# Attention, token mixing and channel mixing on one core: the rows of batch 3 transposed by way of HBM and VectorE instead of TensorE

## The chip, the cores and the metric

The kernel runs on one core of one Trainium2 chip. The metric is the device time of one execution in microseconds (us); the profile's span is some 1.8 us shorter, since it goes from the first to the last instruction. Engines: PE is TensorE (PEld its weight loads), DVE VectorE, ACT ScalarE, POOL GpSimd, SP SyncE, whose queue issues DMAs.

## The reference, cut to what matters

Eight batches, 576 tokens, 8 heads of 64, model width 512. Keys and values are pooled over 8 tokens to 72, attention is computed, and its output x (576 x 512) goes through a token mixing and a channel mixing:

```
xt = x.transpose(0, 2, 1)
h  = np.maximum(xt @ w_tok1, 0.0) @ w_tok2          # mixes tokens
u  = x + h.transpose(0, 2, 1)
h2 = np.maximum(u @ w_ch1, 0.0) @ w_ch2             # mixes channels
return (u + h2).astype(np.float32)
```

The channel mixing contracts over the model width, and the kernel hands u to TensorE with the width on the partitions. The token mixing leaves tokens on the partitions. Each batch's u therefore has to be transposed, 128 x 128 at a time.

## The kernel before

The kernel is written as nine units. Unit n is the channel mixing of batch n: 48 steps, each with two 512-column matmuls, 24 for the first weight (line L512 in the profile of before) and 24 for the second (L534). Unit 8 takes the ninth 64-token piece of every batch, two of which share a tile ("tails"). Into the steps of unit n, a plan weaves the attention of batch n+2 (names with `>`) and the token mixing of batch n+1 (names without). In the timelines each engine's instructions come in the order in which the plan issues them: in run e4 below, VectorE's attention outputs stand behind block transposes that waited 14.2 us.

```
def unit(n, at):
    for i, _ in enumerate(unit_steps(n, ...)):       # two matmuls of the channel mixing, then
        for s in at.get(i, "").split():              # what the plan has at this step
            if s[0] == "l": load(s[1], n + int(s[2])); continue
            ahead = {"<": 0, ">": 2}.get(s[0], 1)
            batches[n + ahead][1][s.lstrip("<>")]()
```

The names that matter: `K V` pool keys and values on GpSimd, `Q0` to `Q3` transpose the queries on VectorE, `kpT` the pooled keys on TensorE, `s0 s1 s2` are score groups, whose exponentials ScalarE takes, `av0` to `av4` the attention outputs (VectorE divides and writes x), `at u` the token mixing, `lq lk lv` load the queries, keys and values of a later batch. There are two ways to transpose u:

```
def uT(c):           # t0..t4: TensorE, then a copy from PSUM
    ps = ps_tr.tile([P, 4, P], BF16, name="pt")                  # this pool has one buffer
    for kk in range(4):
        nc.tensor.transpose(out=ps[:, kk, :], in_=parts(src)[:, kk], identity=ident)
    nc.vector.tensor_copy(out=dst[:, :, o:o + P], in_=ps)

def spill(i):        # M0 M2 M4: u to HBM
    nc.sync.dma_start(out=st["mem"][...], in_=src)
def quads():         # M: back, four DMAs, so that 32x32 blocks lie right
    st["v"] = swap.tile([P, 4 * 5, P], BF16, name="v")           # this pool has one buffer
    for a in range(4):
        nc.sync.dma_start(out=st["v"][32 * a:32 * a + 32, ...],
                          in_=st["mem"][0:n, :, a * P:(a + 1) * P].rearrange("c (i t) f -> t (c i) f", i=4))
def blocks(c):       # T0..T4: VectorE transposes blocks
    nc.vector.transpose(out=dst[...], in_=st["v"][:, 4 * c:4 * c + 4, :]...)
```

Batches 4 to 7 take the second way, batches 1 to 3 the first (batch 0 has one of its own).

The softmax here doesn't subtract the row's maximum and nothing guards it: scores larger than these inputs give would overflow.

Of the kernel before, what the change touches and what calls it, by code (L numbers as in the profile page):

```python
# [20 lines left out]
def kernel(  # L21
# [483 lines left out]
    def unit_steps(n, st):  # L505
# [36 lines left out]
        for a in range(2):  # L542
# [7 lines left out]
            for half in range(2):  # L550
# [9 lines left out]
             11: "lv3", 12: "kpT", 14: "s0", 15: "v1", 19: "s1", 25: "s2", 26: "av0", 27: "av1", 29: "av2",  # L560
             30: ">K1 av4", 31: "av3", 33: "at1", 34: "at0", 35: ">K0", 36: ">V1 u0", 37: "u1", 39: "t0 >V0",
             40: "u2", 41: "t1 u4 u3", 42: "t2", 44: "t3", 46: "t4"}
    SECOND = {0: ">K1 Q0 lq3 kpT Q1 Q2", 1: "lv3", 3: "s0 lk3 >V0", 4: ">K0", 6: "Q3 >V1", 8: "s1", 13: "s2",
              16: "av1 av0", 19: "av2", 20: "av3", 22: "av4", 24: "at1 at0", 26: "u0", 28: ">Q0", 29: "u1", 30: "t0",
              31: "u2", 32: "t1", 33: "u3 t2", 35: "t3", 36: ">Q1", 37: ">kpT", 38: "lq4", 39: ">s0 >Q2",
              40: ">Q3 lv4", 44: ">s1", 45: "lk4"}
    THIRD = {0: ">V0 >K1", 1: "s2", 2: ">K0 >V1", 3: "av0 av1", 6: "av3", 7: "av2", 9: "av4", 10: "at0",
             12: "at1 >Q0", 15: "u0", 16: "u1", 17: "u2 t0", 18: "u4", 19: "t1", 21: "u3", 22: "t2", 24: ">Q1",
             25: "t3", 27: "lq4 >kpT", 28: "lv4", 29: "lk4 >Q3 >s0 >Q2", 32: "t4", 33: ">s1", 38: ">s2", 40: ">av0",
             41: ">av2", 43: ">av1", 45: ">av3", 47: ">av4"}  # L570
    FOURTH = {0: "M4 u4 >K1", 1: "at0 at1 >K0", 3: "u0 >V0", 5: "u1 M0", 6: ">V1", 7: "u2", 8: "u3 M2", 9: "M",
              15: ">kpT >Q1", 17: ">Q0", 22: "lq4", 25: ">Q2", 26: ">s0", 27: "T0", 28: ">Q3 lk4 lv4", 29: "T1",
              32: ">s1 T2", 34: "T3", 37: ">s2", 38: "T4", 39: ">av0", 41: ">av1", 42: ">av2", 45: ">av3", 46: ">av4"}
    LATER = {0: ">K1 at0", 1: "at1", 2: ">V1", 3: "u1 >V0", 5: "u0 u2 u4 >K0", 7: "M0 M4", 9: "u3", 10: "M2", 11: "M",
             14: ">Q0", 17: ">Q1", 20: ">kpT", 22: ">s0", 25: ">Q2", 26: ">Q3", 27: "T0 >s1", 28: "T3", 31: "T2 T1",
             35: ">s2", 37: ">av1 >av0", 38: "T4", 41: ">av2", 45: ">av3", 46: ">av4"}
# [13 lines left out]
    def unit(n, at):  # L590
        if n + 2 < B:
            batches[n + 2][0]()
        for i, _ in enumerate(unit_steps(n, batches[n][2] if n < B else None)):
            for s in at.get(i, "").split():
                if s[0] == "l":
                    load(s[1], n + int(s[2]))
                    continue
                ahead = {"<": 0, ">": 2}.get(s[0], 1)
                s = s.lstrip("<>")
                if n + ahead < B and ((n + ahead) % 2 or s not in ("u4", "t4", "M4", "T4")):  # L600
                    batches[n + ahead][1][s]()

    with tc.manual_schedule(engines={PE, POOLE, DVE, ACT, SYNC}):
# [24 lines left out]
        unit(0, FIRST)  # L628
        unit(1, SECOND)
        unit(2, THIRD)  # L630
        unit(3, FOURTH)
        for n in range(4, B + 1):
# [31 lines left out]
```

## Time and profile before

| | before |
|---|---|
| time, median of 3 first runs | 275.23 us (275.15 to 275.76) |
| span of the profiled run | 273.7 us |
| TensorE busy | 266.1 us, 97% |
| VectorE busy | 52% of the span |
| transposes of u on TensorE (L420) | 56 |
| block transposes on VectorE (L442) | 18 |

The share of busy time does not say what a single instruction costs: matmuls overlap, so 420 of them with a duration of 379 ns each keep TensorE busy for only 101.5 us. The prediction shows the lines of the profile before and reads them.

### The profile page before, as it was taken

How to read it: one execution, taken by the hardware profiler on the slowest of the kernel's cores; microseconds unless marked ns; L12 is line 12 of the kernel's file. 1: busy time of each engine (PE TensorE's matmuls, PEld its weight loads, DVE VectorE, ACT ScalarE, POOL GpSimd, SP SyncE). 2: the span in 40 equal slices, each digit the busy share in tenths (PEclk: the TensorE clock that was granted, in tenths of full speed). 3: DMA queues.
4: the chain of work that ended last, by engine and by line, in shares of the span. 5: the costliest groups of instructions: out<-in, count | busy, mean ns of one | idle time of the engine just before them, and what ended most of it. 6: DMA issues, size and time to landing. Idle time of an engine off the chain costs nothing.

```text
span 273.7 us, 4544 instructions
## 1 busy us (share of the span) xinstructions
PE 266.1 (97%) x1832; PEld 130.4 (48%) x1832; DVE 141.9 (52%) x280; ACT 110.4 (40%) x182; POOL 131.1 (48%) x121
## 2 busy tenths in 40 slices
PE   7799999999999999999999999999999999999994
PEld 3774545544453544454445444544454444444443
DVE  5487677862584666467267627753674062022022
ACT  2443690058306534525641484147413603603600
POOL 8685223999997991899099999300000000000000
PEclk9999999999999999999999999999999999999999
DMA  7999999990976920894399362225223634024024
GB/s 149 195 203 206 205 205 203 227 197 7 175 123 120 220 37 0 140 228 127 77 159 220 94 133 65 61 69 117 52 66 96 125 61 104 0 53 103 2 47 106
DMA packets 36837, 32.68 MB, mean 119 GB/s; under 512 B 14288, under 2 KB 30288, under 8 KB 36816
## 3 DMA queue, kind: packets, MB, share of 16 engines
q0 software_dynamic: 18672, 17.64, 40.7%
q1 hardware_dynamic: 17984, 14.62, 21.1%
q8 instruction: 14, 0.23, 0.3%
q10 hardware_dynamic: 160, 0.13, 0.2%
q14 instruction: 7, 0.06, 0.1%
HBM read 38.21 MB, written 11.80 MB: 183 GB/s over the span
## 4 chain that ended last, share of the span: by engine, by line
PE 89%; DMA 3%; ACT 3%; DVE 2%; POOL 1%; issue 1%; POOLq 0%
PE p L534 33%; PE p L512 32%; PE p L410 6%; PE p L395 6%; PE p L344 3%; PE p L260 3%; DMA vr<-in_v_dram 3%; ACT ex L265 1%; PE pt L420 1%; ACT GT L516 1%; PE p L226 1%; PE p L546 1%; POOL kr L86 1%; PE pt L376 1%; PE p L461 0%
## 5 line engine op out<-in xcount | busy, mean ns | idle before, releaser
L534 PE MATMUL p<-w_ch,GT 128*128 128x512 bf16 x420 | 101.5, 379 | 0.0
L512 PE MATMUL p<-uT,w_ch 128*128 128x512 bf16 x384 | 92.8, 379 | 0.1
L516 ACT ACTIVATE GT<-p 128x512 bf16<-128x512 f32 x108 | 63.8, 598 | 70.4 <-PE p L512 70.0
L512 PEld LDWEIGHTS <-w_ch 128*128 128x128 bf16 x432 | 40.6, 98 | 47.3 <-issue 2.5
L534 PEld LDWEIGHTS <-GT 128*128 128x128 bf16 x420 | 38.0, 98 | 42.0 <-issue 3.3
L520 DVE TENSOR_TENSOR o<-p,u 128x512 f32<-128x512 f32 x32 | 21.9, 685 | 31.6 <-PE p L534 31.2
L265 ACT ACTIVATE ex<-p 72x1024 bf16<-72x1024 f32 (+1 forms) x42 | 31.7, 807 | 13.5 <-PE p L260 13.5
L147 POOL TENSOR_TENSOR t<-t 72x512 f32<-72x512 f32 x24 | 30.4, 1265 | 1.9
L411 DVE TENSOR_TENSOR u<-p,x 128x512 bf16<-128x512 f32 x32 | 21.7, 690 | 14.7 <-PE p L410 14.4
L146 POOL TENSOR_TENSOR t<-kr 72x1024 f32<-72x1024 bf16 x12 | 25.5, 2123 | 6.7 <-DMA kr<-in_k_dram 6.0
L146 POOL TENSOR_TENSOR t<-vr 72x1024 f32<-72x1024 bf16 x12 | 25.5, 2124 | 0.8
L442 DVE STREAM_TRANSPOSE uT<-v 128x512 bf16<-128x512 bf16 x16 | 10.4, 688 | 23.4 <-DMA v<-mem 23.4
L248 DVE STREAM_TRANSPOSE qD<-qb 128x576 bf16<-128x576 bf16 x28 | 20.5, 794 | 0.4 <-DMA qb<-in_q_dram 0.4
L362 DVE TENSOR_TENSOR x<-p,den 128x512 bf16<-128x512 f32 x28 | 19.4, 692 | 1.0
L410 PE MATMUL p<-AT,w_tok 128*128 128x512 bf16 x64 | 18.4, 379 | 0.2 <-ACT GT L516 0.2
L386 ACT ACTIVATE AT<-p 128x512 bf16<-128x512 f32 x7 | 4.2, 597 | 32.2 <-PE p L395 32.2
L344 PEld LDWEIGHTS <-ex 72*128 72x128 bf16 x280 | 13.0, 98 | 7.9 <-DVE x L362 0.7
L356 DVE RECIPROCAL den<-p 128x8 f32<-128x8 f32 (+1 forms) x35 | 7.1, 202 | 15.9 <-PE p L344 15.4
L395 PE MATMUL p<-x,w_tok 128*128 128x512 bf16 x56 | 14.5, 379 | 0.0
L344 PE MATMUL p<-vp,ex 72*128 72x65 bf16 x280 | 14.1, 193 | 0.2 <-ACT ex L265 0.2
L104 POOL DMA_DIRECT2D qb<-in_q_dram x7 | 5.2, 739 | 17.8 <-DVE qD L248 16.2
L260 PE MATMUL p<-qD,kD 32*72 32x512 bf16 (+1 forms) x224 | 11.4, 294 | 0.1
(105 smaller groups left out, 205.4 us busy)
## 6 DMA issues: line engine op xcount, KB each, us to landing
out_dram<-o SPq DMA_DIRECT2D x70, 128.0 KB, 2.4
kr<-in_k_dram POOLq DMA_DIRECT2D x7, 576.0 KB, 13.8
qb<-in_q_dram POOLq DMA_DIRECT2D x7, 576.0 KB, 6.2
vr<-in_v_dram POOLq DMA_DIRECT2D x7, 576.0 KB, 14.1
w_ch<-in_moe_w_ch_dram POOLq DMA_DIRECT2D x6, 512.0 KB, 13.1
mem<-u SPq DMA_DIRECT2D x8, 256.0 KB, 2.1
v<-mem SPq DMA_DIRECT2D x8, 160.0 KB, 3.6
v<-mem SPq DMA_DIRECT2D x8, 128.0 KB, 3.1
```

The lines of the kernel that those rows point to most:

```text
L146: eng.tensor_tensor(out=t4[:, 0:n], in0=t[:, hs, 0:4], in1=t[:, hs, 4:8], op=ALU.add)
L147: eng.tensor_tensor(out=t4[:, 0:n, 0:2], in0=t4[:, 0:n, 0:2], in1=t4[:, 0:n, 2:4], op=ALU.add)
L248: nc.vector.transpose(out=late("qD")[:, g, db].rearrange("m (r j u) -> m u r j", u=2, r=BR), in_=st["qraw"][:, g].rearrange("m (u r d) -> ...
L265: nc.scalar.activation(out=exv[:, a, :, gs.start:gs.stop, n0:n0 + n], in_=pss[a][0:SP, :, 0:len(gs) * n].rearrange("j l (g n) -> j l g n", ...
L344: nc.tensor.matmul(out=halves[h // 4][:, (h % 4) * (D + 1):(h % 4 + 1) * (D + 1)], lhsT=st["ex"][:, h * S + n0:h * S + n0 + P], rhs=st["vp ...
L395: nc.tensor.matmul(out=ps, lhsT=w_tok1[:, c if c < 4 else 4 + par, m * P:(m + 1) * P], rhs=st["x"][:, c, :] if c < 4 else st["xt"], start= ...
L410: nc.tensor.matmul(out=ps, lhsT=w, rhs=a, start=(i == 0), stop=(i == len(mms) - 1))
L411: nc.vector.tensor_tensor(out=dst, in0=ps, in1=x, op=ALU.add)
L512: nc.tensor.matmul(out=ps, lhsT=w_ch1[:, kk, m * P:(m + 1) * P], rhs=uT[:, kk, :], start=(kk == 0), stop=(kk == 3))
L516: nc.scalar.activation(out=GT[:, m, :], in_=ps, func=AF.Relu)
L520: nc.vector.tensor_tensor(out=o_sb, in0=ps, in1=(u_tails if n == B else st["u"])[:, c, :], op=ALU.add)
L534: nc.tensor.matmul(out=pss[c], lhsT=GT[:, m, c * P:(c + 1) * P], rhs=w_ch2[:, m, :], start=(m == 0), stop=(m == NM - 1))
```

## The change

Its intent: take 20 of the transposes of u off the engine that sets the time. Batch 3's `t0` to `t4` go, `M0 M2 M4 M` and `T0` to `T4` come, and around them the plans of units 1 to 3 are set anew. Only the plans differ (cut: the plans of units 0 and 4 to 8 stay as they are).

```
 unit 1
-    SECOND = {0: ">K1 Q0 lq3 kpT Q1 Q2", 1: "lv3", 3: "s0 lk3 >V0", 4: ">K0", 6: "Q3 >V1", 8: "s1", 13: "s2",
-              ... 31: "u2", 32: "t1", 33: "u3 t2", 35: "t3", 36: ">Q1", 37: ">kpT", 38: "lq4", 39: ">s0 >Q2",
-              40: ">Q3 lv4", 44: ">s1", 45: "lk4"}
+    SECOND = {0: "lq3 Q0 kpT", 1: "Q1 Q2 lv3", 3: "s0 >K1", 4: ">V0", 6: "Q3", 7: ">K0 lk3", 8: "s1 >V1", 13: "s2",
+              ... 31: "u2 t1", 32: "u3 t2", 34: "t3", 35: "lq4", 36: ">kpT >Q1", 37: "lv4", 39: ">s0", 40: ">Q2",
+              43: ">Q3", 44: ">s1", 47: "lk4"}
 unit 2
-    THIRD = {..., 15: "u0", 16: "u1", 17: "u2 t0", 18: "u4", 19: "t1", 21: "u3", 22: "t2", 24: ">Q1",
-             25: "t3", 27: "lq4 >kpT", 28: "lv4", 29: "lk4 >Q3 >s0 >Q2", 32: "t4", 33: ">s1", 38: ">s2", 40: ">av0",
-             41: ">av2", 43: ">av1", 45: ">av3", 47: ">av4"}
+    THIRD = {..., 14: "u0", 15: "u2 u1", 17: "M0 u3 M2", 18: "u4 M4", 19: ">Q1", 24: "M", 27: ">Q3 >kpT",
+             29: ">s0 lq4", 30: ">Q2 lk4", 33: ">s1", 34: "lv4", 35: "T0", 36: "T1 T2", 37: ">s2", 38: ">av0",
+             39: ">av2", 41: ">av1 T3", 45: ">av3 T4", 46: ">av4"}
 unit 3
-    FOURTH = {0: "M4 u4 >K1", 1: "at0 at1 >K0", 3: "u0 >V0", 5: "u1 M0", 6: ">V1", 7: "u2", 8: "u3 M2", 9: "M", ...
+    FOURTH = {1: "M4 u4 at0 at1", 2: ">K0 >V0", 3: "u0", 5: "u1 >K1", 7: "u2", 9: "u3 M0", 10: "M2 >V1", 13: "M", ...
```

## The prediction

> **What bounds the kernel now.** I read the page first: part 1 (busy time), then part 2 (the slices), then the chain that ended last. These lines carry it:
>
> ```profile
> PE 266.1 (97%) x1832; PEld 130.4 (48%) x1832; DVE 141.9 (52%) x280; ACT 110.4 (40%) x182; POOL 131.1 (48%) x121
> PE   7799999999999999999999999999999999999994
> GB/s 149 195 203 206 205 205 203 227 197 7 175 123 120 220 37 0 140 228 127 77 159 220 94 133 65 61 69 117 52 66 96 125 61 104 0 53 103 2 47 106
> ```
>
> TensorE is busy from the third slice to the last but one, no other engine passes 52%, and 89% of the chain lies on PE. So work taken off TensorE should come off the time, and work put on VectorE or the queues costs only where TensorE ends up waiting for it. The GB/s row has one more thing for this case: slices of 6.84 us each, and the 15th and 16th (96 to 109 us) move 37 and 0 GB/s.
>
> Busy time of matmuls overlaps, so it does not price one of them. For that I took the timeline of TensorE in the stage that the change rewrites, unit 2 (the channel mixing of batch 2, into which the token mixing of batch 3 is woven), and read from start to start:
>
> ```profile
> 100.22 0.39 PE L420 MATMUL pt<-ident,u 128*128 128x128 bf16 x4
> 100.45 0.59 PE L512 MATMUL p<-uT,w_ch 128*128 128x512 bf16 x2
> 100.88 1.03 PE L410 MATMUL p<-AT,w_tok2t 128*128 128x512 bf16 x4
> ...
> 107.82 0.63 PE L260 MATMUL p<-qD,kD 32*72 32x512 bf16 x8
> 108.38 1.47 PE L534 MATMUL p<-w_ch,GT 128*128 128x512 bf16 x6
> 109.69 0.39 PE L420 MATMUL pt<-ident,u_tails 128*128 128x128 bf16 x4
> 109.91 0.59 PE L534 MATMUL p<-w_ch,GT 128*128 128x512 bf16 x2
> 110.43 0.65 PE L260 MATMUL p<-qD,kD 32*72 32x512 bf16 x8
> ```
>
> Four transposes take 100.45 - 100.22 = 0.23 us (0.22 for the group at 109.69), so 56 ns each; two 512-column matmuls take 100.88 - 100.45 = 0.43 us, so 0.216 us each. No line here has an idle mark: the stage is packed.
>
> **What the Trainium skill says.** "TensorE: Matmul & The Clock Gate", section "Back-to-back issue gap", gives for the isolated gap N / 2.4 + 2.5 ns, which is 56 ns for 128 columns and 216 ns for 512; the trace agrees to the nanosecond. (It also gives about 81 and 131 ns for streams of weight load and matmul; this trace has such streams and shows neither.) Its section "Part 4: PE-mode transpose" has a transpose at 275 to 390 ns; that is a latency, the trace has 219 ns of duration, and on a packed engine only the 56 ns count. "VectorE: DVE Perf Modes", section "The three transpose paths", says that VectorE transposes in 32x32 blocks only; this is why the new path needs a trip through HBM to bring the blocks to the right partitions. "DMA: Bandwidth & Descriptors", section "Specifications", wants 512 B or more per descriptor; the read back has runs of 128 bf16 elements, 256 B. Still the trace has these reads landing in a median of 3.1 and 3.6 us, which is the number I use.
>
> **The change, part by part.** Removed: the five transposing steps of batch 3 (t0 to t3 and the tail t4), 5 x 4 = 20 transposes on TensorE, and their five PSUM copies on VectorE. The instruction order of the changed kernel confirms it: 20 matmuls and 20 weight loads fewer, everything else equal in number. On TensorE, 20 x 56 ns = 1.12 us, all of it on the bounding engine. Beside them:
>
> ```profile
> L421 DVE COPY uT<-pt 128x512 bf16<-128x512 bf16 x12 | 5.0, 420 | 1.3 <-PE pt L420 1.3
> L442 DVE STREAM_TRANSPOSE uT<-v 128x512 bf16<-128x512 bf16 x16 | 10.4, 688 | 23.4 <-DMA v<-mem 23.4
> ```
>
> VectorE loses 5 x 0.42 = 2.1 us and gains 5 x 0.69 = 3.4 us, so +1.3 us in unit 2. In the window 89 to 118.5 us it is busy 18.3 us of 29.5: room enough on average. SyncE's queue gains three spills and four reads (0.36 to 0.5 us of issue each).
>
> Is the new transfer hidden? The last of batch 3's u blocks is written about step 18 of the 48 of unit 2. In the trace of before the fifth comes at 103.9 + 0.7 = 104.6 us with the transposes still woven in; the new plan puts u0 to u4 in steps 14 to 18, so I expect the last near 102 us. Then the last spill 2.1 us, the issue of four reads 2.1 us (as at 129.7 us in unit 3 of before), landing 3 to 4 us: data by about 110 us. The first block transpose stands at step 35. The second phase of unit 2 starts now at 104.8 us and will start some 0.9 us earlier; 12 steps of 0.43 us, the key transposes (0.13) and two score groups (0.56 each) put step 35 at about 110.4. So a small margin, and VectorE also has slack after it. And the DMA engines are idle then: the two empty slices named above. I take this transfer as hidden.
>
> Moved: the plan of unit 2 has the scores of batch 4 at steps 29, 33 and 37 and the first attention product at 38, where before it was 29, 33, 38 and 40. With the transposes gone between them, the order of instructions has 8 channel matmuls between the score groups instead of 6 plus 4 transposes, then 8 instead of 10, then 2 instead of 4. That matters because a score group needs both of its two-bank PSUM buffers back from ScalarE's exponentials:
>
> ```profile
> 108.48 1.93 ACT L265 ACTIVATE ex<-p 72x1024 bf16<-72x1024 f32 x2 [1.02 <-PE p L260]
> 111.10 1.93 ACT L265 ACTIVATE ex<-p 72x1024 bf16<-72x1024 f32 x2 [0.68 <-PE p L260]
> ```
>
> The group at 107.82 frees its second buffer at 108.48 + 1.93 = 110.41, that is 2.59 us after it began; the next group began at 110.43, just behind it. In the new order it could begin 0.56 + 8 x 0.216 = 2.29 us after the first one: a wait of about 0.3 us. The same holds for the third group: about 0.3 us. The first attention product follows the third group after 0.43 us, as it does already in unit 0 at 39.2 to 40.3 us, where the trace has TensorE idle:
>
> ```profile
> 40.30 0.42 PE L344 MATMUL p<-vp,ex 72*128 72x65 bf16 x8 [0.16 <-ACT ex L265]
> ```
>
> I take 0.1 us for it. Together about 0.6 us given back, somewhat less if the groups' own switching time overlaps with the wait.
>
> The plans of units 1 and 3 keep the distances of the score groups (10 and 10, then 12 and 10 matmuls), so I give them no gain or loss, but for small waits in unit 1 of before that the reshuffle may cure: one of 0.19 us at 80.47, where a transpose waits for the only PSUM buffer of its pool, and one of about 0.24 us at 58.7 in a score group that begins late. I credit 0.2 us for the two.
>
> Sum: -1.12 + 0.6 - 0.2 = -0.7 us. 275.23 - 0.7 = 274.5 us.
>
> **The rivals.** (1) The full 1.1 us or more comes off, because the waits of the denser score groups do not appear: 273.7 to 274.1. For it: this looks like a plan that was tuned, and one would not move the groups closer only to lose by it. Against: the 1.93 us of the exponentials do not shrink. (2) The transfer is late: the reads land after step 35, VectorE, which works in order, stands before its block transposes, the attention outputs behind them come late and their PSUM buffers too. For it: the margin is about one microsecond, and in the units that have this path already VectorE idles 23.4 us in all for these reads. Against: TensorE has no idle mark in those units, and the DMA engines are idle at the time. A microsecond of lateness would mostly be absorbed by VectorE, three would cost TensorE one to two: 275.5 to 276.5. (3) VectorE becomes the bound around the end of unit 2: three block transposes in a row (2 us), then five attention outputs of 0.85 us; the third attention product needs the first one's buffer back some 4 us after step 35, and VectorE has it free at about 3.6. Close, worth up to 0.5 us: 275.0. (4) The transposes were hidden anyway: the trace is against it, the matmuls of L420 sit between others with no gap. Then nothing changes: 275.2.
>
> **Range and chances.** All outcomes that I can build lie between 273.6 (all transposes off and all small waits cured) and 276.5 (a late transfer). The three times of before spread by 0.6 us, so the range must be wider than my arithmetic: 273.8 to 275.2. Two per cent is 5.5 us. TensorE's whole idle time is 273.7 - 266.1 = 7.6 us, nearly all in the first 24 us and the last 4, which the change doesn't touch, so faster by 2% is next to impossible; slower by 2% needs a stall of 5.5 us, longer than the whole transfer. Within 2%: 0.985.
>
> **What would show it.** TensorE's matmuls 1812 instead of 1832; L420 at 36 transposes instead of 56; the copies of L421 nine instead of 14, the block transposes 23 instead of 18, with a wait for the reads before the one of batch 3. Between the starts of the score groups in unit 2 about 2.6 us, twice, though the matmuls between would take 2.3; if they are 2.3, rival 1 is right. VectorE's first block transpose of unit 2 near 110 us; if it is past 112 and an attention product has an idle mark behind it, rival 2. The beginning of unit 3 about 0.5 us earlier than before, and from there the same length. Wrong would be a change of over 1.5 us in either direction, which would mean waits in units 1 or 3 that I haven't seen.

## The result, and the profile after

The changed kernel took 274.74 us (median of 6, 274.14 to 275.12) beside 275.40 us of the kernel before. The ratio is 0.9969, 95% interval 0.9952 to 0.9986. Ratios are computed as the mean time of one kernel's runs over that of the other's in the same rounds, so they are not quite the ratio of the medians. Measured twice more, the ratio was 0.9959 (0.9937 to 0.9980) and 0.9983 (0.9951 to 1.0015).

The page of the changed kernel, busy times and traffic:

```profile
PE 265.5 (97%) x1812; PEld 129.5 (47%) x1812; DVE 142.8 (52%) x280; ACT 110.4 (40%) x182; POOL 131.2 (48%) x121
GB/s 140 199 202 206 206 205 208 207 202 97 101 63 164 208 107 157 172 211 107 79 144 220 129 115 74 62 59 118 59 58 96 130 58 103 0 57 99 2 49 105
```

Twenty matmuls fewer, and the two slices that moved 37 and 0 GB/s (the 15th and 16th) now move 107 and 157. The groups of instructions by shape show the same counts as the prediction asked for, 36 transposes, 9 copies, 23 block transposes:

```profile
L442 DVE STREAM_TRANSPOSE uT<-v 128x512 bf16<-128x512 bf16 x20 | 13.0, 686 | 23.9 <-DMA v<-mem 23.9
L421 DVE COPY uT<-pt 128x512 bf16<-128x512 bf16 x8 | 3.3, 418 | 1.4 <-PE pt L420 1.4
L420 PE MATMUL pt<-ident,u 128*128 128x128 bf16 x32 | 3.1, 219 | 0.0
L442 DVE STREAM_TRANSPOSE uT_tails<-v 128x512 bf16<-128x512 bf16 x3 | 2.1, 697 | 0.0
L421 DVE COPY uT_tails<-pt 128x512 bf16<-128x512 bf16 x1 | 0.4, 425 | 0.7 <-PE pt L420 0.7
L420 PE MATMUL pt<-ident,u_tails 128*128 128x128 bf16 x4 | 0.4, 219 | 0.0
```

A difference of 0.7 us between two executions is not far above what single times scatter by. The trace is far sharper, if one compares stages. I take as the start of a unit the start of ScalarE's first operation on its channel blocks (GT, L516 in both). ScalarE's timeline, first the kernel before, at the start of units 2 and 3 (columns: start, duration, engine, instruction, idle time before it):

```profile
88.45 0.60 ACT L516 ACTIVATE GT<-p 128x512 bf16<-128x512 f32 x1 [0.39 <-PE p L512]
...
119.87 0.60 ACT L516 ACTIVATE GT<-p 128x512 bf16<-128x512 f32 x1 [5.58 <-PE p L512]
```

and the changed kernel:

```profile
88.30 0.60 ACT L516 ACTIVATE GT<-p 128x512 bf16<-128x512 f32 x1 [0.40 <-PE p L512]
...
119.03 0.60 ACT L516 ACTIVATE GT<-p 128x512 bf16<-128x512 f32 x1 [6.09 <-PE p L512]
```

Unit 2 lasted 119.87 - 88.45 = 31.42 us and now lasts 119.03 - 88.30 = 30.73 us: 0.69 us less. In the same way unit 1 is 0.06 us longer and unit 3 equal, so the plans and the path together gain 0.63 us. From unit 4 on the two traces differ by 0.00 us per unit. What is left of the difference of the spans lies before unit 1, and there the kernels scattered: the start of unit 1 lay between 57.25 and 58.70 us, and what that comes from is not worked out here. Two further profiles of the changed kernel gave -0.70 us for unit 2 and 0.00 for unit 3 again. The kernel before has one profile, but its unit 2, unchanged in e3 below, took 31.42 us there too. So the unit differences are good to some hundredths of a microsecond, and they carry the rest of this text.

Where the 1.12 us of the 20 transposes went is in TensorE's timeline of unit 2 (changed kernel):

```profile
106.86 0.63 PE L260 MATMUL p<-qD,kD 32*72 32x512 bf16 x8
107.42 1.90 PE L534 MATMUL p<-w_ch,GT 128*128 128x512 bf16 x8
109.25 0.88 PE L260 MATMUL p<-qD,kD 32*72 32x512 bf16 x8
110.06 1.90 PE L534 MATMUL p<-w_ch,GT 128*128 128x512 bf16 x8
111.89 0.38 PE L260 MATMUL p<-qD,kD 32*72 32x64 bf16 x16
112.20 0.60 PE L534 MATMUL p<-w_ch,GT 128*128 128x512 bf16 x2
112.72 0.42 PE L344 MATMUL p<-vp,ex 72*128 72x65 bf16 x8
```

The first score group takes 107.42 - 106.86 = 0.56 us before the next matmul starts, the second 110.06 - 109.25 = 0.81: it waits inside the group, for its second PSUM buffer. The second group of before took 111.02 - 110.43 = 0.59, so 0.22 us are new. The third takes 0.31 us instead of 0.26. The two channel matmuls before the first attention product take 0.52 instead of 0.43, of which 0.01 was there before too. That is 0.22 + 0.05 + 0.08 = 0.35 us. The remaining 0.08 us of the 0.43 given back are earlier, at 98.35 us, where four token-mixing matmuls in a row take 0.95 us instead of 4 x 0.216. And ScalarE, in the same stage:

```profile
107.52 1.93 ACT L265 ACTIVATE ex<-p 72x1024 bf16<-72x1024 f32 x2 [1.02 <-PE p L260]
109.96 1.93 ACT L265 ACTIVATE ex<-p 72x1024 bf16<-72x1024 f32 x2 [0.51 <-PE p L260]
```

The first pair of exponentials ends at 107.52 + 1.93 = 109.45 us, in the middle of the second group. The second pair ends at 109.96 + 1.93 = 111.89 us, the start of the third group: just in time, so there was next to nothing to wait for.

VectorE and the reads (first the answer on the tile that the reads fill, with the times from issue to landing, then VectorE's timeline):

```profile
L436 SPq DMA_DIRECT2D v<-mem x4: 329/504/516, 104.7 to 106.1; - x4
DMA to landing us min/median/max: 2.9/3.7/4.3
```

```profile
111.13 0.69 DVE L520 TENSOR_TENSOR o<-p,u 128x512 f32<-128x512 f32 x1 [2.74 <-PE p L534]
111.74 1.89 DVE L442 STREAM_TRANSPOSE uT<-v 128x512 bf16<-128x512 bf16 x3
...
118.90 0.68 DVE L362 TENSOR_TENSOR xt<-p,den 64x512 bf16<-64x512 f32 x1
```

The last read, issued at 106.1, landed 4.3 us later at 110.4 us. The block transposes began at 111.74, and what they had waited for was not the reads but the output in front of them, which waited for TensorE. So the transfer is hidden, with 1.3 us to spare. The last attention output of the unit was written at 118.90 + 0.68 = 119.58 us, and TensorE's first read of it is at 119.63. That margin is 0.05 us, and it turns out to matter more than the other.

### The profile page after: what moved, and what is told of

The parts are those of the page before. It is cut to its first block, busy times and chain, and to the rows that moved or that the text cites. A ratio compares the mean times of both kernels' runs of the same rounds, so it can differ in the third digit from the quotient of the medians.

```text
span 272.9 us, 4515 instructions
## 1 busy us (share of the span) xinstructions
PE 265.5 (97%) x1812; PEld 129.5 (47%) x1812; DVE 142.8 (52%) x280; ACT 110.4 (40%) x182; POOL 131.2 (48%) x121
## 4 chain that ended last, share of the span: by engine, by line
PE 91%; ACT 3%; DMA 2%; DVE 2%; issue 1%; POOL 0%; POOLq 0%
PE p L534 33%; PE p L512 32%; PE p L410 6%; PE p L395 6%; PE p L344 3%; PE p L260 3%; DMA kr<-in_k_dram 2%; ACT ex L265 1%; ACT GT L516 1%; PE p L226 1%; PE p L546 1%; PE pt L420 1%; PE p L204 1%; PE pt L376 1%; PE p L461 0%
## 5 line engine op out<-in xcount | busy, mean ns | idle before, releaser
L516 ACT ACTIVATE GT<-p 128x512 bf16<-128x512 f32 x108 | 63.8, 598 | 70.3 <-PE p L512 69.9
L411 DVE TENSOR_TENSOR u<-p,x 128x512 bf16<-128x512 f32 x32 | 21.6, 688 | 13.7 <-PE p L410 13.4
L442 DVE STREAM_TRANSPOSE uT<-v 128x512 bf16<-128x512 bf16 x20 | 13.0, 686 | 23.9 <-DMA v<-mem 23.9
L344 PEld LDWEIGHTS <-ex 72*128 72x128 bf16 x280 | 13.1, 98 | 8.3 <-DVE x L362 0.7
## 6 DMA issues: line engine op xcount, KB each, us to landing
vr<-in_v_dram POOLq DMA_DIRECT2D x7, 576.0 KB, 14.9
```

The costliest lines, as they stand in the source:

```text
L344: nc.tensor.matmul(out=halves[h // 4][:, (h % 4) * (D + 1):(h % 4 + 1) * (D + 1)], lhsT=st["ex"][:, h * S + n0:h * S + n0 + P], rhs=st["vp ...
L411: nc.vector.tensor_tensor(out=dst, in0=ps, in1=x, op=ALU.add)
L516: nc.scalar.activation(out=GT[:, m, :], in_=ps, func=AF.Relu)
```

## The experiments

Two theories at the start. Mine: of 1.12 us saved, 0.35 is given back because the score groups stand too close for ScalarE, and the new plans do no more than carry the path. The rival: VectorE, with 1.3 us more to do at the end of unit 2, is what TensorE waits for, and the plans are there for that. The sums below are differences to the kernel before from trace to trace, unit by unit, and the measured ratio.

| run | unit 1 | unit 2 | unit 3 | sum, us | time, median | ratio (95%) |
|---|---|---|---|---|---|---|
| changed kernel | +0.06 | -0.69 | 0.00 | -0.63 | 274.74 | 0.9969 (0.9952 to 0.9986) |
| e1_roomy | +0.06 | -0.67 | +0.86 | +0.25 | 275.99 | 1.0021 (1.0007 to 1.0036) |
| e2_path_only | 0.00 | -0.80 | +1.10 | +0.30 | 275.91 | 1.0020 (1.0001 to 1.0039) |
| e3_plans_only | +0.07 | 0.00 | +0.73 | +0.80 | 276.21 | 1.0032 (1.0012 to 1.0052) |
| e4_late_reads | +0.07 | +15.41 | 0.00 | +15.5 | 291.73 | one run |
| e5_earlier_roomy | +0.07 | -0.48 | 0.00 | -0.41 | 274.99 | 0.9998 (0.9951 to 1.0044) |
| e6_tail_later | +0.07 | -0.67 | +0.26 | -0.34 | 275.34 | one run |
| e7_waits_cured | +0.16 | -0.48 | 0.00 | -0.32 | 275.44 | 1.0006 (0.9978 to 1.0034) |
| e8_late_no_loads | +0.07 | +2.81 | +0.02 | +2.9 | 278.31 | one run |
| e9_both | -0.46 | +9.82 | 0.00 | +9.4 | 284.44 | 1.0303 (1.0270 to 1.0336) |
| e10_query_late | -0.45 | -0.80 | +0.26 | -0.99 | 274.63 | 0.9976 (0.9947 to 1.0005) |
| a0_again (changed kernel) | +0.07 | -0.70 | 0.00 | -0.63 | 274.66 | 0.9959 (0.9937 to 0.9980) |
| a1_again (changed kernel) | +0.07 | -0.70 | 0.00 | -0.63 | 274.92 | 0.9983 (0.9951 to 1.0015) |

The kernel before had medians of 275.4 to 275.5 us beside all of these. All results were correct.

**e1_roomy: give the score groups room.**

```
-  29: ">s0 lq4", 30: ">Q2 lk4", 33: ">s1", ... 37: ">s2", 38: ">av0", 39: ">av2", 41: ">av1 T3", 45: ">av3 T4", 46: ">av4"
+  28: ">s0", 29: "lq4", 30: ">Q2 lk4", 33: ">s1", ... 38: ">s2", 40: ">av0", 41: ">av2 T3", 43: ">av1", 45: ">av3 T4", 47: ">av4"
```

> The changed kernel with the score groups of batch 4 in unit 2 set further apart: ten channel matmuls between each two groups (they had eight) and four before the first attention product (it had two). My theory: TensorE gave back about 0.43 us of the 1.12 us in unit 2, most of it (0.3 to 0.35 us) at the second score group, the third and the first attention product, which wait for ScalarE's exponentials. Then the starts of the groups lie 2.8 us apart without a wait inside a group (the group's own 0.56 us plus ten times 0.216), unit 2 as a whole is 0.3 to 0.4 us shorter than in the changed kernel, and the time is about 274.4 us, or 1.0 us below the kernel before. Rival: TensorE's loss in unit 2 comes from VectorE, which the block transposes keep busy; then spacing the groups leaves unit 2 as long as it is, and the wait moves to the later attention products.

The waits inside the second and third groups went, as expected: 2.82 us from start to start. But unit 2 was no shorter: TensorE now lost 0.26 us before the last attention product and 0.13 us before the first score group, which stands one step closer to the key transposes. And unit 3 lost 0.86 us. TensorE's timeline at the start of unit 3 has the token mixing's read of the last attention output, and VectorE's timeline has that output:

```profile
121.18 0.38 PE L395 MATMUL p<-xt,w_tok 128*128 128x512 bf16 x1 [0.69 <-DVE ex L167]
```

```profile
120.44 0.68 DVE L362 TENSOR_TENSOR xt<-p,den 64x512 bf16<-64x512 f32 x1
121.10 0.07 DVE L166 MEMSET vp<- 72x8 bf16 x1
121.11 0.09 DVE L167 MEMSET ex<- 72x32 uint32 x1
```

The page names the memset as releaser because it is the last of the instructions behind which the semaphore was read; what the matmul reads is xt, ready at 121.12 us. VectorE is busy without a gap from the first attention output on. The rival has this round: room for ScalarE was bought with time that VectorE did not have.

**e2_path_only: the path without the plans.** Unit 2 of before, with the transposes replaced at about the same steps; units 1 and 3 untouched.

```
-  17: "u2 t0", 18: "u4", 19: "t1", 21: "u3", 22: "t2", 24: ">Q1", 25: "t3", ... 32: "t4", 33: ">s1", ... 43: ">av1", 45: ">av3"
+  17: "u2", 18: "u4 M0 M4", 21: "u3 M2", 24: ">Q1 M", ... 33: ">s1", 35: "T0", 36: "T1 T2", ... 43: ">av1 T3", 45: ">av3 T4"
```

> The kernel before with only batch 3's path changed (spills, reads and block transposes in place of its five transposing steps); the plans of units 1 and 3 and all other places in unit 2 as before. My theory: 20 x 56 ns = 1.12 us off TensorE, and about 0.2 us given back, since only the first two score groups come closer (eight channel matmuls between them; ten and four behind, as before). So unit 2 is 0.9 us shorter than before and the time about 274.5 us: as good as the changed kernel or better, so that the adapted plans were not needed. Rival (late transfer): the last spill is issued about three steps later here, so the reads land some 1.5 us later and VectorE's first block transpose waits for them; if that reaches TensorE, an attention product of unit 2 carries an idle mark and the time is 275 us or more.

Unit 2 was 0.80 us shorter, close to my 0.9, with one wait of the size expected in the second score group. But the attention outputs, whose products stand up to two steps later than in the changed kernel (the last one step), came too late for unit 3: the same matmul as in e1 waited 0.95 us (xt ready at 120.22 us), and 1.10 us were lost. The path alone is no faster than the kernel before (1.0001 to 1.0039). So the tighter attention steps of the changed plan, which I had booked as a loss, are one way to make the path pay; e6 below, which keeps the later steps, is another.

**e3_plans_only: the plans of units 1 and 3 without the path.** SECOND and FOURTH of the changed kernel, THIRD of before.

> The kernel before with the adapted plans of units 1 and 3 and nothing else; batch 3 is still transposed on TensorE. My theory: nothing, within 0.1 us of the kernel before (unit 1 of the changed kernel was 0.06 us longer, from the first score group of batch 2 at its start to the last of batch 3; unit 3 the same length). Rival: the adapted plans are worth part of the gain; then this is 0.3 us or more faster than before, and the path itself is worth less than 1.12 us.

Unit 1 came as expected. Unit 3 lost 0.73 us, which I had not: a spill of batch 4 landed after 4.4 us instead of 2.2, the reads were issued 12.5 us after the start of the unit instead of 10.2 in the changed kernel, VectorE's first block transpose waited for them until 137.5 us, and behind it stood the query transpose that the second score group needs. The loads of batch 6 had landed at 126.6 us. What the spill met is in the trace's DMA packets: an instruction fetch of 16 KB began at 129.31 us, while the spill was moving, and took until 131.11; the spill's last 16 KB, a sixteenth of it, moved only from 131.09 us on. The trace does not say which DMA engine carried what, but the times fit. In the changed kernel the fetch comes at 132.19 us, when the spills have landed (129.18). So the 0.73 us probably come from this meeting and not from the order of the plan; no run tests that. The plan of unit 1 brings nothing by itself; of the plan of unit 3, e3 cannot say it.

**e4_late_reads and e8_late_no_loads: what lateness costs.**

```
 e4  unit 2:  -24: "M"  +31: "M"
 e8  the same, and
     unit 2:  -29: "lq4", 30: "lk4", 34: "lv4"
     unit 3:  -2: ">K0 >V0"   +2: ">K0 >V0 lq3 lk3 lv3"      (the same loads, of batch 6)
```

> The changed kernel with the four reads back from HBM issued seven steps later, behind the first two output stores of unit 2 on the same queue, so about 108.8 us instead of 104.7. This measures how much lateness the new path can take. My theory: the block transposes start about 3 us later than 111.7 us, the attention outputs that stand behind them on VectorE come as much later, and since the third attention product (114.5 us) had its buffer back at about 114.4 us there is next to no slack: TensorE loses 2 to 3 us, time 276.5 to 278 us. Rival: VectorE's slack takes it up, less than 0.5 us lost.

> The run with the late reads, but without the loads of batch 6 beside them: these are issued in unit 3 instead. In the late run the reads took a median of 13.1 us to land instead of 3.7, and VectorE waited 14.2 us. Theory: that was because they shared the DMA engines with the loads of batch 6, issued at 109.6 to 112.1 us. Then here they land in about 4 us, VectorE's first block transpose comes at 114 to 115.5 us, and unit 2 is only 2 to 3 us longer than in the changed kernel (what I had expected of lateness alone). Rival: reads behind output stores on the same queue are slow by themselves; then they take 10 us or more here too. Unit 3 may be slow here, since its loads come late on purpose; only unit 2 counts.

In e4 the reads were issued from 109.9 us, 4.3 us later than in the changed kernel, counted from the start of the unit, and here is what became of them (the tile's answer), then VectorE and TensorE:

```profile
DMA to landing us min/median/max: 7.4/13.1/15.2
```

```profile
126.93 1.90 DVE L442 STREAM_TRANSPOSE uT<-v 128x512 bf16<-128x512 bf16 x3 [14.21 <-DMA v<-mem]
```

```profile
129.71 0.62 PE L344 MATMUL p<-vp,ex 72*128 72x65 bf16 x8 [14.11 <-DVE x L362]
130.14 3.55 PE L534 MATMUL p<-w_ch,GT 128*128 128x512 bf16 x8
```

TensorE stood for 14.1 us (the time was 291.73 us where I had expected 276.5 to 278), and then eight matmuls that take 1.9 us elsewhere took 3.55. In a window from 120 to 125 us the granted clock (the column before the last two) is 0.50:

```profile
120.00:125.00 5.00, 0.00 (x0) 0.00 (x0) 0.00 (x0) 0.00 (x0) 4.74 (x4) 0.50 1.06 169
```

The clock fell while the engine idled and was still at 0.50 from 129.7 to 133 us. Without the loads beside them, in e8, the reads were issued from 109.0 us, also 4.3 us later, and landed as they do in the changed kernel (the tile's answer):

```profile
DMA to landing us min/median/max: 3.2/3.8/4.4
```

VectorE began at 115.32 us, and unit 2 was 2.81 + 0.69 = 3.5 us longer than in the changed kernel, a little more than my 2 to 3. So my theory of the long landing holds: the data came 4.7 us later than in the changed kernel, and that cost 3.5 us, about the lateness minus the 1.3 us to spare. The same delay where the reads meet the next loads cost 15.41 + 0.69 = 16.1 us, over four times as much. It is the reads that suffer: the three loads landed 6.3, 11.4 and 14.7 us after their issue in e4, against 6.0, 10.9 and 14.9 in the changed kernel. e4 and e8 are one run each, of unknown state, but the difference is far above any scatter.

**e5_earlier_roomy and e6_tail_later: is it VectorE's queue?**

```
 e6 = e1, and  unit 2:  -45: ">av3 T4"  +45: ">av3"     unit 3:  +8: "<T4"
 e5 = e6 with  27: ">Q3 >s0", 32: ">s1", 37: ">s2", 39: ">av0", 40: ">av2", 41: "T3", 42: ">av1", 44: ">av3", 46: ">av4", 25: ">kpT"
```

> The spaced run with one instruction moved: the block transpose of the tail goes from the end of unit 2 into unit 3. If VectorE's queue is what TensorE waits for, the wait of the token mixing at the start of unit 3 (0.69 us) and the wait of 0.26 us before the last attention product shrink together by about the 0.62 us that the instruction takes: unit 3's loss 0.2 to 0.3 us instead of 0.86. If it is the scores or ScalarE, nothing changes.

> The changed kernel with the score groups ten matmuls apart as in the spaced run, but the whole sequence one step earlier, and the block transpose of the tail (needed only by the last unit) moved from the end of unit 2 into unit 3. Theory now: the spaced run lost 0.86 us at the start of unit 3 because VectorE's queue at the end of unit 2 was behind (the last attention output, which the token mixing reads, was ready at 121.1 us, 0.7 us too late), not because of ScalarE. One step earlier (0.43 us) and one block transpose less (0.62 us) make up for 0.86, so here unit 2 keeps nearly all of the 1.12 us (about 1.0 us shorter than before) and unit 3 is as long as before: 0.9 to 1.0 us below the kernel before at equal start. Rival: the first score group now waits for VectorE or ScalarE instead, and unit 2 is no shorter than in the changed kernel (0.69 us).

Moving one instruction of 0.62 us out of VectorE's queue took 0.86 - 0.26 = 0.60 us from the loss in unit 3. That settles that the start of unit 3 waits for VectorE (e6 is one run; the difference is read in its trace, at a granted clock of 1.00). The wait of 0.26 us before the last attention product stayed; I had not seen that the tail's block transpose stands behind the output that this product waits for. In e5 unit 3 is as before, but unit 2 shortened by 0.48 us only: the rival came true, for its second score group now began 0.28 us late, waiting for a query transpose that stood behind an output on VectorE. The wait before the last attention product, here 0.28 us, stayed too.

**e7_waits_cured: waits in unit 1.** The plan of e5 with `>Q0` of batch 2 at the end of unit 0, `t2` and `t3` a step later, `>Q3` at step 40.

> The previous plan plus three moves in units 0 and 1 for waits that both kernels have: one query transpose of batch 2 earlier, so that its first score group finds it done (0.24 us), two transposing steps of batch 2 one step later, so that the single PSUM buffer is free (0.19 us), and the last query transpose of batch 3 as early as it was before (0.06 us). Theory: 0.4 us less in unit 1 than in the changed kernel, together 1.4 us below the kernel before at equal start: about 274.0 us. Rival: VectorE or the load of the next query takes the wait over, unit 1 unchanged.

The query transpose brought its 0.27 us. The later transposes pushed the wait for the single PSUM buffer to the key transposes and made it larger (TensorE's timeline of this run):

```profile
80.97 0.29 PE L195 MATMUL pt<-ident,kp 72*128 72x72 bf16 x4 [0.46 <-DVE uT L421]
```

Unit 1 became 0.16 us longer than before: a miss.

**e9_both and e10_query_late: all of it together.**

```
 e9  unit 1: token mixing of batch 2 a step earlier (28: "t0", 30: "u2 t1", 31: "u3", 32: "t2", 34: "t3"), ">Q0" in unit 0, ">Q3" at 40
     unit 2: the plan of e5, with  -30: ">Q2 lk4"  +28: ">Q2", 30: "lk4"    and  -35: "T0"  +34: "T0"
 e10 e9, with unit 2's places as in e6 (26: ">kpT", 27: ">Q3", 28: ">s0", 30: ">Q2 lk4", 33: ">s1", 34: "T0 lv4", ...)
```

> The earlier spaced plan with what its trace still showed mended: the second score group waited 0.28 us for a query transpose that stood behind an output on VectorE (now ahead of it), the last attention product 0.28 us for VectorE's backlog (now the first block transpose stands ahead of the second output, in time that VectorE spent idle), and unit 1 with the early query transpose (0.27 us, seen) and all token mixing of batch 2 one step earlier so that neither its transposes nor the key transposes wait for the one PSUM buffer (0.2 us; the last try moved that wait to the key transposes and doubled it). Theory: unit 1 0.4 us shorter than before, unit 2 1.0 us, unit 3 equal: 1.4 us below the kernel before at equal start and 0.8 below the changed one, ratio 0.994 to 0.997. Rival: TensorE finds another wait in the place of each cured one, and it is no faster than the changed kernel.

> The previous plan with the third query transpose of batch 4 back behind the first output on VectorE, where the changed kernel has it, and the score groups at the places of the spaced run. In the previous run moving it ahead released the loads of batch 6 at 104.9 us instead of 108.7, in the middle of the reads, whose last then landed at 119.3 us instead of 110.4; TensorE stood 8.2 us for it. Theory: with the transpose late the loads start at 109 us or later, the reads land by 110.5 us, and the rest of the plan comes to its worth: unit 1 0.46 us shorter than before (seen in the previous run), unit 2 1.0 us, unit 3 equal, ratio to the kernel before 0.994 to 0.997 and about 0.8 us below the changed kernel. Rival: the early block transposes or the spread score groups cost TensorE by themselves; then unit 2 stays at 0.7 us or less and only unit 1's 0.46 us come.

> The changed kernel itself once more, beside the next one on the same chip. Theory: 0.6 us below the kernel before in units 1 to 3 (unit 1 +0.06, unit 2 -0.69, unit 3 0.00, from the start of one unit's first exponentiated channel block to the next, as in its first profile), the rest of any difference from the beginning, before the first channel matmul, which varied by some 0.5 us from profile to profile in all kernels; so a ratio of 0.996 to 0.999. Rival: the ratio of 0.9969 of the first measurement owed something to its chip or hour; then it is 1.000 here with the same units in the trace.

> The changed kernel beside the previous one on the same chip, to compare the two: units 1 to 3 in the trace as in its other profiles (+0.06, -0.69, 0.00 us against the kernel before), ratio 0.996 to 0.998, so the previous kernel should be 0.2 to 0.4% faster than this one if its theory holds, and equal or slower if its rival does.

In e9 unit 1 gained 0.46 us, more than expected, and unit 2 lost 9.82. I had moved one query transpose two steps forward. GpSimd's queue shows what hung on it, here the load of the next queries in e9:

```profile
104.94 0.75 POOL L104 DMA_DIRECT2D qb<-in_q_dram  x1 [1.67 <-DVE qD L248]
```

and in the changed kernel:

```profile
108.69 0.76 POOL L104 DMA_DIRECT2D qb<-in_q_dram  x1 [3.21 <-DVE qD L248]
```

The load waits for the last reader of the buffer that it overwrites, and with it wait the loads of keys and values behind it. Moved forward, the transpose let all three start from 104.9 us on, in the middle of the reads, the last of which landed after 13.4 us. VectorE's first block transpose waited for it:

```profile
119.32 0.71 DVE L442 STREAM_TRANSPOSE uT<-v 128x512 bf16<-128x512 bf16 x1 [11.22 <-DMA v<-mem]
```

TensorE stood 8.2 us for that, and its granted clock was 0.50 from 119 to 125 us. In the changed kernel the transpose stands late, behind an output that waits for TensorE, and holds the loads back until the reads are nearly done. In e10 it stands late again (and the score groups have e6's places, so two things differ from e9): the reads landed within 4.0 us, unit 1 kept 0.45 us, unit 2 was 0.80 us shorter. But the two waits of e6 at the end of unit 2 came back unchanged (0.25 and 0.26 us), although the first block transpose stood earlier: VectorE then idled 0.88 us before its first attention output and was again busy without a gap from there on. The early block transpose did not cure it; the chain of attention outputs is itself too late. In the trace e10 is 0.36 us shorter over units 1 to 3 than the changed kernel. The times, 0.9976 beside 0.9983, can't tell the two apart, so I do not claim a version that beats it. The two repeats of the changed kernel came as expected, 0.9959 and 0.9983.

## Why the prediction was right or wrong

The time (274.74 us) lies in the range and near the predicted 274.5. Step by step:

- **TensorE bounds, and 20 transposes are worth 1.12 us.** Right. Unit 2 is 0.69 us shorter with 0.43 us of waits accounted for, and 0.69 + 0.43 is 1.12. All counts came as told. One reading was wrong without harm to the sum: before, there were not 6 but 8 channel matmuls between the first two score groups (6, the four transposes, then 2).
- **The transfer is hidden.** Right: data at 110.4 us where the prediction said about 110. The block transposes followed at 111.74 rather than 110.4, because they stood behind an output, and no attention product shows a wait for them.
- **0.6 us given back at the score groups and the first attention product.** The mechanism was right, the size too large: 0.22, 0.05 and 0.08 us, so 0.35. The sign I had named, 2.6 us from start to start twice, came as 2.39 and 2.64. The term that failed is the third group's 0.3 us. I computed it as if the second group were as short as the first; but the wait falls inside the second group and lengthens it by itself, and by the time of the third group ScalarE is just done (111.89 us on both). A further 0.08 us in the token mixing was not foreseen.
- **0.2 us credited for waits in unit 1.** Wrong. Both stayed: the first score group of batch 2 took 0.82 us in place of 0.56 (0.83 before), and a transpose waited 0.19 us, now at 78.5 us. Unit 1 became 0.06 us longer, by the second score group of batch 3 (0.62 us in place of 0.56). It needed other moves than those made; e9 and e10 show 0.45 us for them. This error of 0.26 us and the previous one of 0.17 us (0.60 against 0.43) nearly cancelled: -0.7 predicted, -0.63 in the trace. That the two are so close is luck.
- **The plans bring no gain or loss of their own.** True of unit 3 in the changed kernel, to 0.06 us of unit 1, and misleading as a reason. With the path and the old places of the attention outputs, e2 lost the whole gain.
- **Rival 3, VectorE at the end of unit 2**, which I gave up to 0.5 us: it costs nothing in the changed kernel, by 0.05 us of margin, and 0.86 and 1.10 us in e1 and e2, where the attention outputs stand up to two steps later. The place where I looked for it (the third product's buffer) was not where it bit; that was the last output, read by the next unit.
- **Rival 2, a late transfer.** It did not come. I had sized it at one to two us for three us of lateness. e8 fits that size, with 3.5 us for data 4.7 us later and 1.3 us to spare. e4 does not: 16 us where the reads meet the next loads. There I had taken the landing time as fixed.

## What to carry to other kernels

Taking work off the bounding engine paid here only where the engine that got it had room at the place where it got it: VectorE's 52% over the span said nothing about the end of unit 2, where its queue was full and the next unit waited for its last entry. Before moving an instruction that reads a load's buffer, look at what load waits for it; a late reader can be what keeps two transfers apart. And compare traces stage by stage: differences of 0.1 us were plain between starts of stages, when the times of whole runs could not tell 0.4 us.

## What the Trainium skill lacked or had wrong

- "TensorE: Matmul & The Clock Gate", section "Back-to-back issue gap", gives about 81 and 131 ns per matmul as what streams of weight load and matmul reach, and calls the isolated formula wrong for them. Here such streams, read from start to start in the timelines above, ran at 56 ns for 128 columns and 216 ns for 512, as the formula has it.
- I found no page with a number for what it costs a transfer in 256-byte runs to share the DMA engines with larger loads: four reads landed after a median of 3.7 us when the next batch's loads began 2.6 us behind them, 13.1 us beside these loads, and 3.8 us again with the loads moved away.
- Nor one that tells to look for loads held back by a buffer's last reader: in e9 one query transpose, moved forward among other changes, released the loads 3.75 us earlier (104.94 for 108.69 us), and unit 2 became 9.8 us longer than before.
